# A second row buffer for the token scatter, 18 unread products, and a later copy of the experts' token numbers

## The chip, the cores and the metric

The kernel runs on one core of a Trainium2 chip. The metric is the device time of one execution in microseconds (us), the median of several runs. Profiles come from one execution that the hardware profiler recorded. Engines are named as in the profile: PE is TensorE's matrix products (PEld its weight loads), DVE is VectorE, ACT is ScalarE, POOL is GpSimd, SP is the engine whose queue issues most of the DMAs.

## What is computed

Three layers follow each other: attention that keeps the 32 largest scores of a row (2 batches, 8 heads, 576 positions, 64 per head), a dense layer with a cosine (1152 tokens, 512 to 2048 and back), and a mixture of 8 experts of which each token takes one.

```python
scores = scale * np.matmul(q, k.transpose(0, 1, 3, 2))
kth = np.partition(scores, -top_k, axis=-1)[..., -top_k:-top_k + 1]
scores = np.where(scores >= kth, scores, -1000000000.0)
attn = np.exp(scores - np.max(scores, axis=-1, keepdims=True))
attn = attn / (np.sum(attn, axis=-1, keepdims=True) + 1e-09)
x = np.matmul(attn, v)            # reordered to 1152 tokens x 512
h = x @ w_in
x = (h * np.cos(h)) @ w_out
...
expert_idx = np.argmax(x @ w_gate, axis=1)
# a token goes to row counts[e] of its expert's list, in order of token number
h = np.maximum(np.einsum('ecd,edf->ecf', disp, w1), 0.0)
y = np.einsum('ecf,efd->ecd', h, w2)
out[i] = gate_w[i] * y[expert_idx[i], pos[i]]
```

## The kernel before

**Stages.** Attention and the dense layer work on 9 tiles of 128 tokens, numbered 0 to 8 (tile 4 holds the ends of both batches). The dense layer takes the tiles in the groups [0], [1, 2], [3, 4], [5, 6] and [7, 8]. For a group, `layer_in` (L662) writes 512 columns of the hidden layer into `h`, ACT copies them to `hs` (L691), DVE and ACT form the cosine in `ur` (L695, L712), POOL multiplies (L720), and `layer_out` (L723) adds 16 products per tile into `x2` (L729).

**Routing.** `route` (L735) takes a finished tile of `x2`: ACT copies it into a row tile `xr` (L742), PE transposes it into `pt` (L660), ACT copies that to `gT` (L744), PE multiplies by the gate weights into `av` (L748), DVE picks the expert (L751 to L756), ACT takes the exponentials (L768), and DVE writes the gate weight beside the row (L760). `place` (L773) counts on PE how many earlier tokens chose each expert (L786), DVE makes row addresses `slot` from that (L789 to L792), and POOL scatters the 128 rows of `xr` to `xs` in DRAM by an indirect DMA (L795). Tile 4 has a row tile of its own, `xr4`, and is placed last, since it needs the counts of both batches. `largest` (L804) adds up all counts and lets DVE note whether a list is too long (L815 to L817, L831).

All tiles but 4 share the ring `xr`, and the ring `gT` and the PSUM ring `av` have one buffer each too.

**Experts.** `gather` (L949) loads an expert's rows from `xs` into `xg` by four DMAs, after all nine scatters. PE transposes them into `xp` (L964, L965), ACT and DVE split them into two parts `xgs` (L967, L968), and `expert_in` (L971) and `expert_out` (L997) run the two layers (products at L979, L981 and L1010). The result rows are scattered to the output (L1016) by token numbers, which DVE copies as integers from the gathered rows into `ti` (L959). Weights are loaded into `raw2` or `raw3` and split by ACT (L944) and DVE (L946).

**Order.** The class `Plan` records every operation with a cost, a rank and its dependencies; `emit` walks through time with these costs, picks for each engine the operation that can start first (the rank decides among those within 0.02 us), and writes out one fixed order per engine. Ring buffers are handed out there: an operation that needs a new buffer waits in the plan until one is free. On the chip every engine runs its queue strictly in this order and waits by semaphores. `forward` is written out twice: with `paired` true, which is what runs here, and as an exact version behind a test that isn't entered with these inputs.

The rings that the change touches, and the place of the token copy:

```python
    ring("xr", "mx", [128, RW], F32)
    ring("xr4", "mx", [128, RW], F32, tag="raw")
...
        P.dma(1.0, 1.6, ld, r=[("xs", t) for t in range(9)], w=[kx])
        P.op("dve", 0.1, lambda: DVE.tensor_copy(T["ti", e], T[kx][:, :, DM + 1]), r=[kx], w=[("ti", e)])
...
        R("rank", 90.0 + 10 * e - prm["ga"])
        gather(e)
```

Of the kernel before, what the change touches and what calls it, by code (L numbers as in the profile page):

```python
# [7 lines left out]
F32 = mybir.dt.float32  # L8
F32R = mybir.dt.float32r
BF = mybir.dt.bfloat16  # L10
# [9 lines left out]
T = B * S  # L20
DM = H * D
# [4 lines left out]
RW = 520  # L26
# [225 lines left out]
def forward(ctx, lasting, tc, kq, vn, vs_, w_in, w_out, w_gate, w1, w2, out, paired):  # L252
    nc = tc.nc
    PE, ACT, DVE, POOL, SP = nc.tensor, nc.scalar, nc.vector, nc.gpsimd, nc.sync
    prm = PRM if paired else FULL
    P = Plan(prm["tb"])
    T = P.T
# [13 lines left out]
    def ring(name, pool, shape, dtype, bufs=1, tag=None, gate=None):  # L271
        P.ring(name, lambda: pools[pool], shape, dtype, bufs, tag, gate)
# [5 lines left out]
    tri = lasting("tri", [128, 128], BF)  # L278
    ones = lasting("ones", [128, 128], BF)
    right = lasting("right", [128, 128], BF)  # L280
    iota8 = lasting("iota8", [128, 8], F32)
    tok = lasting("tok", [128, 9], F32)
    far = lasting("far", [128, 9], F32)
# [8 lines left out]
    counts = lasting("counts", [128, NE + 3], I32)  # L292
# [4 lines left out]
    CONST, MASKS = ("ident",), ("masks",)  # L297

    def iota(t, pattern, base, cm):
        POOL.iota(t, pattern=pattern, base=base, channel_multiplier=cm, allow_small_or_imprecise_dtypes=True)  # L300
# [14 lines left out]
    def masks():  # L315
        def go():
            iota(iota8, [[1, 8]], 0, 0)
            iota(tok[:, 0:4], [[128, 4]], 0, 1)
            iota(tok[:, 5:9], [[128, 4]], S, 1)
            iota(tok[0:64, 4:5], [[1, 1]], 512, 1)  # L320
            iota(tok[64:128, 4:5], [[1, 1]], S + 512, 1)
            iota(spare, [[1, 1]], int(OUT_OF_RANGE), 1)
            POOL.memset(ones, 1.0)
            POOL.tensor_scalar(far, tok, 1.0, OUT_OF_RANGE, op0=OP.add, op1=OP.mult)
            POOL.memset(right, 0.0)
            POOL.memset(right[:, 64:128], 1.0)
        P.op("pool", 1.2, go, w=[MASKS])
        P.dma(0.5, 0.3, lambda: SP.dma_start(wg, w_gate.rearrange("(c p) e -> p c e", p=128)), w=[("wg",)])
# [323 lines left out]
    ring("ur", "mx", [128, 2, 512], F32, 2, tag="ur")  # L652
    ring("nn", "mx", [128, 512], F32)
    ring("gT", "mx", [128, 512], F32)
    ring("xr", "mx", [128, RW], F32)
    ring("xr4", "mx", [128, RW], F32, tag="raw")

    def transposes(kp, src):
# [145 lines left out]
    def largest():  # L804
        kp = ("av", "total")

        def count():
            for t in range(9):
                PE.matmul(T[kp][:, 0:NE], ones, onehot[:, t], start=(t == 0), stop=(t == 8))
        P.op("pe", 0.1, count, r=[("pick", t) for t in range(9)] + [MASKS], w=[kp])  # L810

        m8, over, un = small[:, 8, 16:24], small[:, 8, 28:29], small[:, 8, 29:30]

        def tally():
            DVE.max(m8, T[kp][:, 0:NE])  # L815
            DVE.tensor_scalar(over, m8[:, 0:1], float(MAIN), None, op0=OP.is_gt)
            DVE.tensor_copy(counts[:, 0:NE], T[kp][:, 0:NE])  # L817
        P.op("dve", 0.3, tally, r=[kp, ("slot", 8)], w=[("counts", 0)])
        if not paired:
            P.op("dve", 0.1, lambda: DVE.tensor_copy(counts[:, NE:NE + 1], over), r=[("counts", 0)], w=[("counts", 1)])  # L820
            return
        kd = ("av", "doubts")
        P.op("dve", 0.4, lambda: (DVE.tensor_scalar(edge, edge, 0.0, 0.0, op0=OP.is_ge, op1=OP.add, accum_out=doubts[:, 0:1]),
                                  DVE.tensor_scalar(turns, turns, FEWER, 0.0, op0=OP.is_lt, op1=OP.add, accum_out=doubts[:, 1:2]),
                                  DVE.tensor_tensor(out=doubtb, in0=doubts[:, 0:1], in1=doubts[:, 1:2], op=OP.add)),
             r=[("edge", s) for s in range(NSTEPS)] + [("turns", t, g) for q in groups for t in q[:1] for g in range(2 * len(q))], w=[("doubts", 0)])
        P.op("pe", 0.1, lambda: PE.matmul(T[kd][:, 0:1], ones, doubtb, start=True, stop=True), r=[("doubts", 0), MASKS],
             w=[kd])
        P.op("dve", 0.2, lambda: (DVE.tensor_copy(counts[:, NE + 1:NE + 2], T[kd][:, 0:1]), DVE.tensor_copy(un, T[kd][:, 0:1])),
             r=[kd], w=[("counts", 2)])  # L830
        P.op("dve", 0.1, lambda: DVE.tensor_tensor(out=counts[:, NE:NE + 1], in0=un, in1=over, op=OP.add),  # L831
             r=[("counts", 0), ("counts", 2)], w=[("counts", 1)])


    R = P.__setattr__
    R("rank", -3.0)
# [30 lines left out]
    for q in groups:  # L867
        t, n = q[0], len(q)
# [24 lines left out]
                 table="exp")  # L893
    place(4)
    largest()
    all_first = range(len(P.ops))
    att = [i for i in all_first if any(k[0] in P.rings and P.rings[k[0]][0]() is pools["at"] for k in P.ops[i]["tiles"])]

# [29 lines left out]
    def wkey(q, e, i, a):  # L928
        return (q + "2" if e % 2 == 0 else q, (e, i, a))
# [19 lines left out]
    def gather(e):  # L949
        kx = ("xg", e)  # L950

        def ld():
            SP.dma_start(T[kx][:, 0, :], xs[e * CAP:e * CAP + 128, :])

            SP.dma_start(T[kx][:, 1, 0:DM], xs[e * CAP + 128:e * CAP + 256, 0:DM])
            for a in range(2):
                SP.dma_start(T[kx][64 * a:64 * a + 64, 1, DM:RW], xs[e * CAP + 128:e * CAP + MAIN, DM:RW])
        P.dma(1.0, 1.6, ld, r=[("xs", t) for t in range(9)], w=[kx])
        P.op("dve", 0.1, lambda: DVE.tensor_copy(T["ti", e], T[kx][:, :, DM + 1]), r=[kx], w=[("ti", e)])  # L959
        for c in range(4):  # L960
            kp, ks = ("xp", (e, c)), ("xgs", (e, c))

            def tr(c=c, kp=kp):
                PE.transpose(T[kp][:, 0:128], T[kx][:, 0, c * 128:(c + 1) * 128], ident)  # L964
                PE.transpose(T[kp][:, 128:256], T[kx][:, 1, c * 128:(c + 1) * 128], ident)  # L965
            P.op("pe", 0.25, tr, r=[kx], w=[kp], duty=0.5)
            P.op("act", 0.25, lambda kp=kp, ks=ks: ACT.activation(T[ks][:, 0], T[kp][:, 0:MAIN], AF.Copy), r=[kp], w=[ks])  # L967
            P.op("dve", 0.27, lambda kp=kp, ks=ks: DVE.tensor_tensor(  # L968
                out=T[ks][:, 1], in0=T[kp][:, 0:MAIN], in1=T[ks][:, 0], op=OP.subtract), r=[kp], w=[ks])
# [27 lines left out]
    def expert_out(e, a):  # L997


        kp, ko = ("yp", (e, a)), ("ot", (e, a))  # L1000
        for fc in range(8):
            ka, kb = wkey("wh", e, 4 + fc // 2, fc % 2), wkey("wl", e, 4 + fc // 2, fc % 2)

            def mm(fc=fc, ka=ka, kb=kb):
                h = T["hc", (e, fc)]
                hi, lo = h[:, 0:128], h[:, MAIN + 64:2 * MAIN]
                both = h[:, 128:256]
                uses = ((both, T[ka]), (both, T[kb])) if a else ((hi, T[ka]), (hi, T[kb]), (lo, T[ka]))
                for n, (x, w) in enumerate(uses):
                    PE.matmul(T[kp], x, w, start=(fc + n == 0), stop=(fc == 7 and n == len(uses) - 1))  # L1010
            P.op("pe", 0.463 if a else 0.695, mm, r=[ka, kb, ("hc", (e, fc))], w=[kp])

        rows = 64 if a else 128

        def scatter():
            st = POOL.indirect_dma_start(out=out, out_offset=bass.IndirectOffsetOnAxis(ap=T["ti", e][0:rows, a:a + 1], axis=0),  # L1016
                                         in_=T[ko][0:rows, :], in_offset=None, bounds_check=B * S - 1, oob_is_err=False)
            for x in outs:
                tc.declare_no_dep(st.ins, x.ins, reason="distinct tokens")
            outs.append(st)  # L1020

        def gates(r):
            return T["xg", e][r, a, DM:DM + 1]
        if a == 0:
            P.op("act", 0.55, lambda: ACT.activation(T[ko], T[kp], AF.Copy, scale=gates(slice(0, 128))),  # L1025
                 r=[kp, ("xg", e)], w=[ko])
        else:
            P.op("act", 0.55, lambda: ACT.activation(T[ko][0:64, :], T[kp][64:128, :], AF.Copy, scale=gates(slice(64, 128))),
                 r=[kp, ("xg", e)], w=[ko])
            P.op("dve", 0.6, lambda: DVE.scalar_tensor_tensor(  # L1030
                T[ko][0:64, :], T[kp][0:64, :], gates(slice(0, 64)), T[ko][0:64, :], op0=OP.mult, op1=OP.add),
                r=[kp, ("xg", e)], w=[ko])
        P.op("pool", 1.05, scatter, r=[ko, ("ti", e), ("filled",)], w=[("done", e, a)], lat=3.5)
# [103 lines left out]
```

## Time and profile before

| what | us |
|---|---|
| median of 3 runs | 698.27 (697.89 to 698.58) |
| the profiled execution | 697.17 |
| its span, first to last instruction | 695.4 |
| PE busy in it | 587.0 (84%) |
| DVE busy | 552.0 (79%) |
| ACT busy | 494.3 (71%) |
| POOL busy | 265.8 (38%) |

The profiled execution is 1.1 us below the median. Three stretches follow each other in it: up to about 410 us DVE and ACT are busy nearly all the time with attention; from there to 501 us PE is, with the last groups of the dense layer; from 530 us on PE is again, with the experts. Between 501 and 530 us no engine is busy for long: routing of the last tiles, their scatter, and the first gather lie there, one behind the other. Time in this stretch is read from the chain of waits and from the engines' own sequences, not from busy shares.

### The profile page before, as it was taken

What the parts mean: (1) busy time and instruction counts of PE and PEld (TensorE: products, weight loads), DVE (VectorE), ACT (ScalarE), POOL (GpSimd) and SP (SyncE); (2) the same over time, 40 slices, a digit from 0 to 9 for tenths busy, and PEclk for the clock granted to TensorE, in tenths of its full rate; (3) what the DMA queues carried; (4) which work ended last, traced back from release to release, by engine and by line L of the source; (5) the groups of instructions that cost most, each with busy time, mean ns of one, the idle gap of its engine ahead of it and who ended that gap; (6) DMA issues with size and microseconds to landing.
All of it is one profiled execution on the core that took longest, in us unless ns stands there. A gap on an engine that the chain in (4) does not pass through costs nothing.

```text
span 695.4 us, 11074 instructions
## 1 busy us (share of the span) xinstructions
PE 587.0 (84%) x3611; PEld 431.9 (62%) x3611; DVE 552.0 (79%) x1654; ACT 494.3 (71%) x1004; POOL 265.8 (38%) x316
## 2 busy tenths in 40 slices
PE   3333577799999999989999899999926999999994
PEld 1122355545776755866756567667425888999993
DVE  5999999999999999999999962555223888889630
ACT  4676998999799989787877764566313777778631
POOL 3466675677445545464544541322110101101111
PEclk9995658999899999999999999999956999999997
DMA  9543552064131201000000002353113677787300
GB/s 348 189 151 124 163 168 92 1 231 182 56 101 39 71 6 39 20 16 17 1 1 1 0 17 87 126 169 135 61 46 123 224 250 251 266 269 259 108 18 16
DMA packets 30786, 77.28 MB, mean 111 GB/s; under 512 B 4606, under 2 KB 4606, under 8 KB 30720
## 3 DMA queue, kind: packets, MB, share of 16 engines
q1 hardware_dynamic: 28976, 71.73, 30.7%
q0 software_dynamic: 1744, 4.76, 1.8%
q8 instruction: 30, 0.49, 0.3%
q14 instruction: 36, 0.29, 0.1%
HBM read 64.57 MB, written 12.69 MB: 111 GB/s over the span
## 4 chain that ended last, share of the span: by engine, by line
PE 40%; DVE 35%; ACT 15%; DMA 3%; issue 3%; POOL 1%; SPq 1%; POOLq 0%; DVEq 0%; ACTq 0%
PE yp L1010 11%; DVE W L513 9%; DVE C L517 8%; PE x L729 8%; PE hp L979 7%; DVE C L509 5%; PE hp L981 3%; ACT Sp L561 2%; DVE W L522 2%; ACT pen L556 2%; DVE wt L405 2%; ACT Sp L570 2%; ACT Sp L494 2%; PE h L684 2%; DVE Sp L574 2%
## 5 line engine op out<-in xcount | busy, mean ns | idle before, releaser
L729 PE MATMUL x<-wo,hs 128*128 128x512 f32 x288 | 138.2, 603 | 0.0
L559 POOL TENSOR_TENSOR Sp<-Sp,pen 128x576 f32<-128x576 f32 x72 | 98.9, 1373 | 63.9 <-ACT pen L556 63.3
L513 DVE MAX8 W<-C 128x8 f32<-128x288 f32 x288 | 118.2, 446 | 0.6
L946 DVE TENSOR_TENSOR wl<-raw,wh 128x512 fp32r<-128x512 f32 x128 | 89.9, 739 | 35.4 <-ACT wh L944 34.9
L517 DVE MATCH_REPLACE8 C<-W,C 128x288 f32<-128x288 f32 x216 | 93.8, 440 | 0.0
L589 PE MATMUL pt<-ident,Sp 128*128 128x128 f32 x324 | 56.4, 304 | 39.1 <-ACT Sp L570 32.5
L482 PE MATMUL S<-kq 64*128 64x288 f32 x256 | 57.8, 533 | 28.7 <-ACT Sp L494 19.8
L589 PEld LDWEIGHTS pt<-ident,Sp 128*128 128x128 f32 x324 | 40.0, 153 | 66.9 <-ACT Sp L570 42.1
L944 ACT ACTIVATE wh<-raw 128x512 fp32r<-128x512 f32 x128 | 74.0, 621 | 9.9 <-DMA raw<-in_w_dram 6.9
L684 PE MATMUL h<-xh,wh 128*128 128x256 f32 x256 | 78.1, 305 | 0.5 <-ACT hs L691 0.4
L979 PE MATMUL hp<-xgs,wh 128*128 128x384 f32 x256 | 76.3, 368 | 0.0
L729 PEld LDWEIGHTS x<-wo,hs 128*128 128x128 f32 x288 | 49.0, 190 | 43.5 <-issue 42.7
L1016 POOL DMA_INDIRECT out_dram<-ot,ti x16 | 16.6, 1035 | 152.8 <-ACT ot L1025 121.6
L685 PE MATMUL h<-xl,wh 128*128 128x256 f32 x256 | 71.9, 281 | 0.0
L686 PE MATMUL h<-xh,wl 128*128 128x256 f32 x256 | 71.8, 281 | 0.0
L1010 PE MATMUL yp<-wh,hc 128*128 128x512 f32 x192 | 68.4, 400 | 0.0
L509 DVE TENSOR_TENSOR C<-Sp 128x576 f32<-128x576 f32 x72 | 65.1, 904 | 3.0 <-ACT Sp L494 2.2
L720 POOL TENSOR_TENSOR hs<-hs,ur 128x512 f32<-128x512 f32 x36 | 48.4, 1356 | 46.4 <-ACT ur L712 45.0
L561 ACT ACTIVATE Sp<-Sp,tb 128x576 f32<-128x576 f32 x72 | 55.6, 773 | 14.2 <-POOL Sp L559 14.0
L981 PE MATMUL hp<-xgs,wl 128*128 128x192 f32 x256 | 65.3, 255 | 0.0
L556 ACT ACTIVATE pen<-Sp,tb 128x576 bf16<-128x576 f32 x72 | 55.2, 767 | 6.3 <-POOL tb L549 5.5
L591 ACT ACTIVATE PT<-pt 128x384 f32<-128x384 f32 x108 | 48.6, 483 | 12.2 <-PE pt L589 12.0
(138 smaller groups left out, 1365.8 us busy)
## 6 DMA issues: line engine op xcount, KB each, us to landing
raw<-in_w_dram SPq DMA_DIRECT2D x64, 512.0 KB, 3.8
wraw<-in_w_out_dram SPq DMA_DIRECT2D x16, 512.0 KB, 3.8
wraw<-in_w_in_dram SPq DMA_DIRECT2D x16, 512.0 KB, 4.0
xs<-z SPq DMA_DIRECT2D x1, 4680.0 KB
kq<-in_kq_dram SPq DMA_DIRECT2D x8, 576.0 KB, 5.7
v<-in_vn_dram SPq DMA_DIRECT2D x8, 320.0 KB, 6.2
v<-in_vs_dram SPq DMA_DIRECT2D x8, 320.0 KB, 3.3
out_dram<-z SPq DMA_DIRECT2D x1, 2304.0 KB
```

The lines of the kernel that those rows point to most:

```text
L509: DVE.tensor_tensor(out=T["C", s], in0=x[:, :, 0:HS], in1=x[:, :, HS:S], op=op)
L513: P.op("dve", 0.365, lambda r=r, i=i: DVE.max(T["W", s][:, i, LIST[r]:LIST[r] + 8], T["C", s][:, i, :]), r=[("C", s, i)], w=[("W", s, i)])
L517: P.op("dve", 0.42, lambda r=r, i=i: DVE.match_replace(T["C", s][:, i, :], T["W", s][:, i, LIST[r]:LIST[r] + 8], T["C", s][:, i, :], NEG), ...
L559: P.op("pool", 1.34, lambda i=i, kp=kp: POOL.tensor_tensor(out=T["Sp", s][:, i, :], in0=T["Sp", s][:, i, :], in1=T[kp], op=OP.subtract), r ...
L589: PE.transpose(T[kp][:, c * 128:(c + 1) * 128], P2[:, cc * 128:(cc + 1) * 128], ident)
L684: PE.matmul(o, hi, a, start=(kc == 0), stop=False, skip_group_check=True)
L729: P.op("pe", 0.86, lambda f=f, a=a: PE.matmul(T["x2", t], T[kh][:, a:a + 128], T["wo", 0][:, f, :], start=(f == 0), stop=(f == 15)), r=[kh ...
L944: P.op("act", 0.52, lambda a=a, hi=hi: ACT.activation(T[hi], T[kr][:, a * 512:(a + 1) * 512], AF.Copy), r=[kr], w=[hi])
L946: P.op("dve", 0.6, lambda a=a, hi=hi, lo=lo: DVE.tensor_tensor(out=T[lo], in0=T[kr][:, a * 512:(a + 1) * 512], in1=T[hi], op=OP.subtract), ...
L979: PE.matmul(T[kp][:, 0:2 * MAIN], T[ka][:, c:c + 128], x.rearrange("p a n -> p (a n)"), start=(kc == 0), stop=False, skip_group_check=True)
L981: PE.matmul(T[kp][:, 0:MAIN], T[kb][:, c:c + 128], x[:, 0], start=False, stop=(kc == 3), skip_group_check=True)
L1010: PE.matmul(T[kp], x, w, start=(fc + n == 0), stop=(fc == 7 and n == len(uses) - 1))
```

## The change

It has three parts.

- The ring `xr` gets two buffers.
- A new tile `awake` of 128 x 512 zeros in bfloat16 is set by POOL at the start, and a new function `stay_awake` puts 18 products of `ones` with it behind `largest`, in a tile of the ring `av`. Nothing reads the result. They depend on the first tally on DVE.
- The copy of the token numbers into `ti` is taken out of `gather` and recorded at the first half (`a == 0`) of `expert_out`, so that its rank is 96 + 10e instead of 90 + 10e - 4.016 in `paired`.

```diff
+    awake = lasting("awake", [128, 512], BF)
...
             POOL.memset(ones, 1.0)
+            POOL.memset(awake, 0.0)
...
-    ring("xr", "mx", [128, RW], F32)
+    ring("xr", "mx", [128, RW], F32, 2)
...
+    def stay_awake(n):
+
+        kp = ("av", "awake")
+
+        def mm():
+            for _ in range(n):
+                PE.matmul(T[kp], ones, awake, start=True, stop=True)
+        P.op("pe", 0.214 * n, mm, r=[MASKS, ("counts", 0)], w=[kp])
...
     place(4)
     largest()
+    if paired:
+        stay_awake(18)
...
         P.dma(1.0, 1.6, ld, r=[("xs", t) for t in range(9)], w=[kx])
-        P.op("dve", 0.1, lambda: DVE.tensor_copy(T["ti", e], T[kx][:, :, DM + 1]), r=[kx], w=[("ti", e)])
...
         kp, ko = ("yp", (e, a)), ("ot", (e, a))
+        if a == 0:
+            P.op("dve", 0.1, lambda: DVE.tensor_copy(T["ti", e], T["xg", e][:, :, DM + 1]), r=[("xg", e)], w=[("ti", e)])
```

The plan then writes other orders. ACT's queue at the end of routing; `xr_4963` and `xr_5005` are the row tiles of tiles 7 and 8. Before:

```order
L742 ACTIVATE xr_4963<-x2_4675 128x512
L744 ACTIVATE gT_4969<-pt_4968 128x512
L768 ACTIVATE small_87<-small_87 128x8
L742 ACTIVATE xr_5005<-x2_4754 128x512
L744 ACTIVATE gT_5010<-pt_5009 128x512
L768 ACTIVATE small_87<-small_87 128x8
L967 ACTIVATE xgs_5107<-xp_5101 128x192
```

Now (`xr_4965` is that of tile 7, `xr_4976` that of tile 8):

```order
L744 ACTIVATE xr_4965<-x2_4677 128x512
L744 ACTIVATE xr_4976<-x2_4762 128x512
L746 ACTIVATE gT_4971<-pt_4970 128x512
L746 ACTIVATE gT_4993<-pt_4992 128x512
L770 ACTIVATE small_88<-small_88 128x8 x2
L979 ACTIVATE xgs_5128<-xp_5122 128x192
```

The two tiles are now taken together, step by step, instead of one after the other.

PE's queue from the last product of the dense layer to the experts' first transposes (rows of the counts left out). Before:

```order
L729 MATMUL x2_4754<-wo_138,hs_4927 128x512 x2
L660 MATMUL pt_4968<-ident_75,xr_4963 128x128 x4
L748 MATMUL av_4975<-wg_86,gT_4969 128x8 x4
L786 MATMUL av_4987<-onehot_88,tri_76 128x8
...
L660 MATMUL pt_5009<-ident_75,xr_5005 128x128 x4
L748 MATMUL av_5016<-wg_86,gT_5010 128x8 x4
L786 MATMUL av_5028<-onehot_88,tri_76 128x8
...
L964 MATMUL xp_5101<-ident_75,xg_5085 128x128
```

Now:

```order
L731 MATMUL x2_4762<-wo_140,hs_4935 128x512 x2
L662 MATMUL pt_4970<-ident_75,xr_4965 128x128 x4
L750 MATMUL av_4981<-wg_87,gT_4971 128x8 x4
L662 MATMUL pt_4992<-ident_75,xr_4976 128x128 x4
L788 MATMUL av_4999<-onehot_89,tri_76 128x8
...
L750 MATMUL av_5018<-wg_87,gT_4993 128x8 x4
L788 MATMUL av_5030<-onehot_89,tri_76 128x8
...
L842 MATMUL av_5079<-awake_79,ones_77 128x512
...
L976 MATMUL xp_5122<-ident_75,xg_5106 128x128
```

Tile 8's transposes moved ahead of tile 7's count, and the 18 products stand between the counts and the first expert's transposes. Tile 6's transposes and gate products moved ahead as well, between products of the last group's `h`.

DVE's queue where the experts begin; `xg_5085` and `xg_5090` are the rows of experts 0 and 1. Before:

```order
L831 TENSOR_TENSOR counts_90<-small_87 128x1
L959 CAST ti_5099<-xg_5085 128x2
L968 TENSOR_TENSOR xgs_5107<-xp_5101,xgs_5107 128x192
L959 CAST ti_5112<-xg_5090 128x2
L968 TENSOR_TENSOR xgs_5110<-xp_5104,xgs_5110 128x192
L968 TENSOR_TENSOR xgs_5121<-xp_5114,xgs_5121 128x192
```

Now (experts 0 and 1 are `xg_5106` and `xg_5111`):

```order
L833 TENSOR_TENSOR counts_91<-small_88 128x1
L1014 CAST ti_5120<-xg_5106 128x2
L980 TENSOR_TENSOR xgs_5128<-xp_5122,xgs_5128 128x192
L1014 CAST ti_5133<-xg_5111 128x2
L980 TENSOR_TENSOR xgs_5131<-xp_5125,xgs_5131 128x192
L980 TENSOR_TENSOR xgs_5142<-xp_5135,xgs_5142 128x192
```

Both copies stand where they stood; those of the experts 2 to 6 moved back by four instructions, that of expert 7 stayed, and SP's queue is unchanged.

## Rows read from the trace of the kernel before

**Rows 1.** The chain of waits between 494 and 530 us: start, us, what.

```profile
494.19 6.97 PE x L729 x16
...
506.76 2.81 DMA xs<-xr,slot
509.67 0.61 ACT xr L742
...
517.41 4.03 DMA xs<-xr,slot x2
...
525.32 3.59 DMA xg<-xs
529.03 0.17 DVE ti L959
```

**Rows 2.** Busy time of PE, PEld, DVE, ACT, POOL by stretch, then PE's clock.

```profile
480.00:500.00 20.00, 20.00 (x73) 10.96 (x72) 8.03 (x15) 7.28 (x13) 5.45 (x6) 1.00 0.29 95
...
560.00:640.00 80.00, 80.00 (x467) 72.39 (x466) 68.40 (x196) 63.59 (x160) 8.35 (x8) 1.00 0.78 262
```

**Rows 3.** ACT in order of time: start, us, what, in brackets the idle time before.

```profile
499.62 0.60 ACT L742 ACTIVATE xr<-x 128x512 f32<-128x512 f32 x1 [8.19 <-PE x L729]
501.70 0.60 ACT L744 ACTIVATE gT<-pt 128x512 f32<-128x512 f32 x1 [1.48 <-PE pt L660]
...
509.67 0.60 ACT L742 ACTIVATE xr<-x 128x512 f32<-128x512 f32 x1 [4.78 <-DMA xs<-xr,slot]
```

**Rows 4.** PE in order of time, from the last routing to the first expert.

```profile
501.00 0.60 PE L660 MATMUL pt<-ident,xr 128*128 128x128 f32 x4
502.35 1.06 PE L748 MATMUL av<-wg,gT 128*128 128x8 f32 x8 [0.75 <-ACT gT L744]
...
512.18 1.88 PE L748 MATMUL av<-wg,gT 128*128 128x8 f32 x8 [0.75 <-ACT gT L744]
...
524.40 0.45 PE L964 MATMUL xp<-ident,xg 128*128 128x128 f32 x1 [7.21 <-DMA xg<-xs]
...
529.51 0.47 PE L964 MATMUL xp<-ident,xg 128*128 128x128 f32 x1 [2.28 <-DVE xgs L968]
...
533.68 0.57 PE L979 MATMUL hp<-xgs,wh 128*128 128x384 f32 x1
...
534.21 0.57 PE L979 MATMUL hp<-xgs,wh 128*128 128x384 f32 x1
```

**Rows 5.** DVE in order of time, in the same stretch.

```profile
505.30 0.15 DVE L789 SCALAR_TENSOR_TENSOR small<-av,onehot 128x8 f32<-128x8 f32 x1
...
517.51 0.16 DVE L817 CAST counts<-av 128x8 int32<-128x8 f32 x1
...
526.05 0.17 DVE L959 CAST ti<-xg 128x2 int32<-128x2 f32 x1 [8.27 <-DMA xg<-xs]
...
529.03 0.17 DVE L959 CAST ti<-xg 128x2 int32<-128x2 f32 x1 [2.55 <-DMA xg<-xs]
```

**Rows 6.** Stretches of half a microsecond around two changes of PE's clock.

```profile
504.00:504.50 0.50, 0.04 (x2) 0.04 (x2) 0.43 (x3) 0.01 (x1) 0.00 (x0) 0.58 0.00 0
...
534.50:535.00 0.50, 0.50 (x4) 0.50 (x4) 0.19 (x1) 0.28 (x1) 0.00 (x0) 0.70 0.00 0
```

**Rows 7.** Stretches of one microsecond around an earlier fall of the clock.

```profile
81.00:82.00 1.00, 0.34 (x4) 0.00 (x0) 1.00 (x4) 1.00 (x4) 0.19 (x1) 1.00 0.00 0
...
84.00:85.00 1.00, 0.00 (x0) 0.00 (x0) 1.00 (x7) 0.82 (x2) 1.00 (x2) 0.62 0.83 160
```

**Rows 8.** The chain of waits, 34 products of 512 columns.

```profile
543.97 7.91 PE yp L1010 x34
```

**Rows 9.** Tile 6's row copy on ACT.

```profile
466.84 0.60 ACT L742 ACTIVATE xr<-x 128x512 f32<-128x512 f32 x1 [1.42 <-DMA xs<-xr,slot]
```

**Rows 10.** Waits between 425 and 500 us: total, times, longest.

```profile
ACT wh L944 <- DMA raw<-in_w_dram: 6.9, 5, 2.7
```

**Rows 11.** The stretch after the masks, at the start of the program.

```profile
3.00:4.00 1.00, 0.00 (x0) 0.00 (x0) 0.00 (x0) 0.00 (x0) 0.00 (x0) 1.00 1.00 361
```

## The prediction

> **What bounds the kernel now.** I read the busy time by stretch first: PE has no idle moment from 480 to 500 us, nor in the 80 us from 560 to 640 [rows 2]. A microsecond saved on another engine there is worth nothing. Between these stretches the chain of waits [rows 1] shows one thing after another: the last product of `x2` ends at 494.19 + 6.97 = 501.16, tile 7 is routed and its scatter lands (506.76 + 2.81), only then ACT copies tile 8 at 509.67, tile 8 goes the same way, its scatter is issued at 517.41, the gathers follow, and the experts' products begin behind 529.5. Here a microsecond off the chain is a microsecond off the end, because what follows (gathers, weight loads behind them in SP's queue, experts) moves as one block.
>
> The sequence on ACT shows the one wait that a second row tile addresses: ACT stands for 4.78 us before tile 8's copy, until the scatter of the first row tile has landed [rows 3]. Tile 8's products had ended 8.5 us before (501.16 against 509.67).
>
> **The second row tile.** What it removes is not the 4.78 us alone, since tile 7's own routing also lay ahead of tile 8's. I follow the new order until tile 8's gate product, which started at 512.18 [rows 4].
> - Tile 7's copy stays at 499.62, tile 8's starts when PE has ended: 501.16 plus 0.17, the lag between the end of tile 7's last product (499.45, two products of tile 8 earlier, each two instructions of 6.97 / 16 = 0.43) and tile 7's copy. It ends at 501.93.
> - Tile 7's `gT` stood at 501.70 [rows 3] and now goes behind that copy: 0.2 us late. Its gate product moves from 502.35 to 502.55 and ends at 503.6.
> - Tile 8's transposes follow on PE, 0.60 us as tile 7's [rows 4]: 504.2. Its `gT` on ACT, 0.60 more with 0.1 of lag: 504.9.
> - `av` has one buffer. So tile 8's gate product also waits until DVE has read tile 7's count, at 505.30 + 0.15 before [rows 5]. With the 0.2 us it is 505.7, later than 504.9, and decides.
>
> Gain: 512.18 - 505.7 = **6.5 us**. From there to the gathers the steps and their order are those of before. Bounds: by 506 us PE ran at half clock before (below); if it still ran at the full level, the gate product would take 1.06 instead of 1.88 us [rows 4], which makes 7.3. If each of the four hand-overs lost another 0.25 us, it would be 5.5. POOL has no conflict: the scatters of 7 and 8 are then some 4 us apart, and one took 2.81 to land.
>
> The second buffer also lets tile 6 be routed earlier. Its copy waited for a scatter until 466.84 [rows 9]; now its transposes stand among PE's products from about 461 us. PE's work stays the same and fills its time, so this is worth 0, unless a product waits (last rival).
>
> The `awake` memset on POOL lies at the start, where no engine but the DMAs has work from 3 to 4 us [rows 11]. 0.
>
> **The 18 products.** No row shows a product of bfloat16 zeros. The nearest are products of 512 columns: 7.91 / 34 = 0.23 us each at the full level of the clock (2.4 GHz) [rows 8]. At the half level (1.2 GHz) the experts' first products come at 534.21 - 533.68 = 0.53 us for 384 + 192 columns [rows 4], thus 0.47 for 512. 18 of them take 4.2 or 8.5 us. They wait for DVE's cast of the counts, which ended at 517.67 [rows 5], and the first rows of an expert were there at 524.40 [rows 4]: a pause of 6.7 us, which moves along unchanged.
>
> Which level do they find? The clock fell at 504.08 (of the half microsecond from 504.0 a share of 0.16 was at the full level, mean 0.58) and rose at 534.80 [rows 6], 5.3 us after PE began to work steadily at 529.51. So the products start at half clock. If it rises 5.3 us after their start too, 5.3 / 0.47 = 11.3 are done by then, the other 6.7 take 1.5 us, and they end 6.8 us after their start, when the rows arrive. The transposes may lose some tenths, up to 8.5 - 6.7 = 1.8 us if the clock does not rise. Neither is on the path: DVE's copy of expert 1's token numbers waits until 529.03 [rows 5], the second split and the last transposes (529.51) stand behind it, and these transposes before had waited 2.28 us for DVE [rows 4].
>
> What they could give is the half clock at the experts' begin. From 529.51 to 534.80 PE ran at half level; at full level the same work takes half of 5.3, so **at most 2.6 us**. But it must hold from the end of the 18 products to 529.85 in old times, that is from 517.7 + 6.8 = 524.5 on, 5.3 us with only eight transposes in it. The rows say that it does not. After 501.16 four transposes and eight gate products ran, and the clock fell 2.9 us later [rows 6]; after 81.34 nothing ran, and it fell at 84.24, also 2.9 us later [rows 7]. I take **0**, and keep 2.6 for the range.
>
> One rule stands on the other side. The Trainium skill, page "TensorE: Matmul & The Clock Gate", section "Seeing it yourself", shows a run in which the clock fell 5.2 us after the last matmul. By that it would just about reach the experts' first product, and the sum would be 9.1 instead of 6.5 us. The rows of this case, 2.9 us twice, are the nearer evidence, but it gives the first rival more weight.
>
> **The copy of the token numbers.** One DVE instruction of 0.17 us per expert. The wait that matters is 2.55 us for expert 1's rows, in front of expert 0's second split [rows 5]. In the new queue that copy stands at the same place, behind expert 0's first split; the new rank changed nothing there, since the plan believed the rows to be there and DVE had nothing else to start. For the experts 2 to 6 the copy goes back by four instructions, in a stretch that PE fills [rows 2]. 0 in both.
>
> **Sum.** 6.5 + 0 + 0. Against the profiled execution: 697.17 - 6.5 = 690.7. That execution was 1.1 us faster than the median of its runs, and nothing in the chain above explains that, so I set the sum against the median: 698.27 - 6.5 = **691.8**. With the bounds of 5.5 and 7.3 it is 691.0 to 692.8.
>
> **Rivals.**
> 1. *The clock holds until the experts begin.* For it: the skill's 5.2 us, and the eight transposes in between, half a microsecond each at half level. Against it: the two falls after 2.9 us. 691.8 - 2.6 = 689.2. Chance 0.17.
> 2. *A wait takes the place of the one removed.* Tiles 7 and 8 meet in the single `av` and `gT`, and ACT's exponential of tile 7 stands behind tile 8's `gT`. If tile 8's gate product had to wait until tile 7's address is complete and the scatter is issued (506.76 [rows 1], 507 with the lag), the gain is 512.18 - 507 = 5.2, or 4 with a microsecond lost in the hand-overs: 693 to 694.3, 693.7 in the middle. Against it: the waits by data end at 505.7. Chance 0.07.
> 3. *Nothing gained.* Should the gathers hang on something else that ends at 521.7 as before, the time stays at 698.3. Against it: the chain names only the two scatters [rows 1]. Chance 0.02.
> 4. *Slower: PE's full stretch opens.* From 480 to 500 us PE was never idle [rows 2], so an idle microsecond there is added to the end. ACT's copies of tile 6 (row tile and `gT`, 1.2 us) now precede its copies of `h`, and `h` has one buffer. ACT also waits for weights, up to 2.7 us at a time [rows 10]. If that longest wait fell ahead of all four remaining copies of `h`, PE would lose 10.8 us: 698.27 - 6.5 + 10.8 = 702.6. It decides from 6.5 + 1.4 = 7.9 us on. Against it: three or more products of 0.87 us stand between the groups of `h` as cover. Chance 0.03.
>
> **How the numbers follow.** The forecast has the remaining 0.71. About 0.2% (1.4 us) is what a measurement of this kernel can tell from no change. Forecast and the first two rivals (0.95) lie beyond it on the fast side; I add a little to both others for what I overlooked. The range takes in the first rival with 0.4 us below it for the spread of the runs, and reaches to 693.4 above, past the forecast's own bound and half way into the second rival.
>
> **What would show it.** Right: in the new profile ACT's two row copies stand side by side near 500 and 501 us, without a wait for a scatter; the scatter of tile 8 is issued near 511 instead of 517.4; the 18 products run from about 511 to 518, the first half or more at half clock; PE's clock is at half again when the experts' products begin near 523, and rises about 5 us later; DVE still waits some 2.5 us for expert 1's copy. The clock step is wrong if those products come every 0.29 us from the first on. The first step is wrong if tile 8's gate product starts later than 506.5. The forecast as a whole would be wrong if `x2`'s last product ended later than 501.5 us.

## The result and the profile after

The changed kernel takes 691.59 us (median of 4 runs, 690.42 to 692.5), the kernel before beside it 698.14. The ratio is 0.9905, with a 95% interval of 0.9886 to 0.9923: 6.6 us or 0.95% faster, against a forecast of 691.8 in a range of 688.8 to 693.4. The profiled execution took 692.26, its span 690.5.

In that execution `x2` ended 1.8 us later than in the one shown of before (what goes with it, below). So places are compared by their distance from the end of `x2`'s last product, which was 501.16 and is 502.92. The chain of waits (start, duration, what; the answer to [rows 1]):

```profile
495.93 6.99 PE x L731 x16
502.94 0.60 ACT xr L744
...
505.72 0.60 ACT gT L746
...
507.29 1.86 PE av L750 x8
...
512.43 4.02 DMA xs<-xr,slot x2
516.70 0.33 SPq L966
...
520.33 3.61 DMA xg<-xs
524.06 0.17 DVE ti L1014
```

The scatter of tile 7, which stood in the chain of before ahead of tile 8's copy, is gone from it. From the end of `x2` to tile 8's gate product it is 4.37 us (before 11.02), to its scatter 9.51 (16.25). That takes 6.65 us off the gate product and 6.74 off the scatter. What follows kept its length: the gathers are issued 4.27 us behind the scatter (before 4.28). ACT in order of time (start, duration, line, what, in brackets the idle time before; [rows 3]):

```profile
501.22 0.60 ACT L744 ACTIVATE xr<-x 128x512 f32<-128x512 f32 x1 [8.21 <-PE x L731]
502.94 0.60 ACT L744 ACTIVATE xr<-x 128x512 f32<-128x512 f32 x1 [1.12 <-PE x L731]
503.43 0.59 ACT L746 ACTIVATE gT<-pt 128x512 f32<-128x512 f32 x1
505.72 0.60 ACT L746 ACTIVATE gT<-pt 128x512 f32<-128x512 f32 x1 [1.70 <-PE pt L662]
```

The second copy waits for PE alone. The 4.78 us for the scatter are not there. PE in the same stretch ([rows 4]):

```profile
504.08 1.06 PE L750 MATMUL av<-wg,gT 128*128 128x8 f32 x8 [0.74 <-ACT gT L746]
...
507.29 1.84 PE L750 MATMUL av<-wg,gT 128*128 128x8 f32 x8 [0.55 <-DVE small L791]
...
512.74 0.59 PE L842 MATMUL av<-awake,ones 128*128 128x512 bf16 x1 [0.53 <-DVE counts L819]
513.55 4.94 PE L842 MATMUL av<-awake,ones 128*128 128x512 bf16 x16 [0.22 <-issue]
519.51 0.30 PE L976 MATMUL xp<-ident,xg 128*128 128x128 f32 x1 [1.02 <-DMA xg<-xs]
...
524.54 0.48 PE L976 MATMUL xp<-ident,xg 128*128 128x128 f32 x1 [2.76 <-DVE xgs L980]
...
524.88 0.67 PE L991 MATMUL hp<-xgs,wh 128*128 128x384 f32 x1
525.35 0.36 PE L993 MATMUL hp<-xgs,wl 128*128 128x192 f32 x1
525.51 0.57 PE L991 MATMUL hp<-xgs,wh 128*128 128x384 f32 x1
...
526.04 0.57 PE L991 MATMUL hp<-xgs,wh 128*128 128x384 f32 x1
```

The 18 products (17 of them are in the records) end at 518.49, a microsecond before the rows they fill the time for. The products of the experts' first layer, `hp`, still come in pairs 0.63 and 0.53 us apart, the half level of the clock. DVE's copy of expert 1's token numbers waits as before ([rows 5]: 2.55 us):

```profile
506.97 0.16 DVE L791 SCALAR_TENSOR_TENSOR small<-av,onehot 128x8 f32<-128x8 f32 x1
...
524.06 0.17 DVE L1014 CAST ti<-xg 128x2 int32<-128x2 f32 x1 [2.78 <-DMA xg<-xs]
```

Half microseconds around the four changes of PE's clock, and PE in the stretch before (busy time of PE, PEld, DVE, ACT, POOL, then PE's clock; [rows 2, 6]):

```profile
480.00:500.00 20.00, 20.00 (x66) 10.27 (x65) 8.04 (x15) 7.84 (x14) 5.75 (x8) 1.00 0.32 105
...
505.50:506.00 0.50, 0.12 (x2) 0.00 (x0) 0.43 (x4) 0.28 (x1) 0.00 (x0) 0.98 0.00 0
...
516.00:516.50 0.50, 0.50 (x3) 0.25 (x2) 0.00 (x0) 0.00 (x0) 0.00 (x0) 0.78 0.01 0
...
523.00:523.50 0.50, 0.00 (x0) 0.00 (x0) 0.00 (x0) 0.00 (x0) 0.00 (x0) 0.54 0.97 352
529.50:530.00 0.50, 0.50 (x3) 0.50 (x3) 0.16 (x1) 0.31 (x1) 0.00 (x0) 0.63 0.00 0
```

A clock of 0.78 in a half microsecond means that a share of 0.56 of it was at the full level (0.56 x 1 + 0.44 x 0.5). So the clock fell at 505.98, 3.1 us after `x2`'s last product, rose at 516.22, fell again at 523.04, 4.55 us after the last of the 18 products, and rose at 529.87. The experts began 1.8 us after the second fall. PE has no idle moment from 480 to 500, as before.

### The profile page after: what moved, and what is told of

Read it like the earlier page. It is cut to its first block, busy times and chain, and to the rows that moved or that the text cites. A ratio compares the mean times of both kernels' runs of the same rounds, so it can differ in the third digit from the quotient of the medians.

```text
span 690.5 us, 11105 instructions
## 1 busy us (share of the span) xinstructions
PE 594.1 (86%) x3628; PEld 436.3 (63%) x3629; DVE 550.1 (80%) x1654; ACT 494.4 (72%) x1004; POOL 265.6 (38%) x317
## 4 chain that ended last, share of the span: by engine, by line
PE 43%; DVE 30%; ACT 19%; issue 2%; DMA 2%; POOL 1%; SPq 1%; POOLq 0%; DVEq 0%; ACTq 0%
PE yp L1024 11%; PE x L731 8%; DVE W L515 8%; PE hp L991 8%; DVE C L519 7%; DVE C L511 4%; PE hp L993 3%; ACT Sp L572 3%; ACT pen L558 3%; ACT Sp L563 3%; PE h L686 2%; ACT Sp L496 2%; DVE W L524 2%; PE h L687 2%; PE h L688 2%
## 5 line engine op out<-in xcount | busy, mean ns | idle before, releaser
L959 DVE TENSOR_TENSOR wl<-raw,wh 128x512 fp32r<-128x512 f32 x128 | 88.3, 727 | 33.5 <-ACT wh L957 32.5
```

What stands on the lines that cost most here:

```text
L959: P.op("dve", 0.6, lambda a=a, hi=hi, lo=lo: DVE.tensor_tensor(out=T[lo], in0=T[kr][:, a * 512:(a + 1) * 512], in1=T[hi], op=OP.subtract), ...
```

## The experiments

Theory: the second row tile is the whole gain, by the wait that left the chain; the 18 products and the token copy are worth nothing, each because one wait of DVE (2.78 us for expert 1's rows in this execution) stands in the same place. Rivals: the products carry part of it, or the copy does.

Ratios are to the kernel before, measured beside each run on the same chip; a ratio is not the quotient of the two medians named below, from which it differs by up to 0.2%. The runs of one kernel range over 0.7 to 5.8 us, so a difference of one microsecond is read from the traces. All times in the table are us from one trace each:

| kernel | ratio, 95% interval | `x2` end to gate product of tile 8 | `x2` end to first `hp` | first `hp` to PE's last product | clock at first `hp` |
|---|---|---|---|---|---|
| before | 1 | 11.02 | 28.69 | 156.50 | half, for 4.95 |
| copy_moved | 1.0001 (0.9983 to 1.0019) | 11.01 | 28.07 | 157.05 | half, for 6.0 |
| products | 1.0004 (0.9987 to 1.0020) | 11.02 | 27.83 | 155.57 | half, for 2.9 |
| after | 0.9905 (0.9886 to 0.9923) | 4.37 | 21.96 | 156.53 | half, for 5.0 |
| two_rows | 0.9911 (0.9890 to 0.9932) | 4.38 | 20.45 | 155.69 | half, for 2.9 |
| after_36 | 0.9859 (0.9837 to 0.9882) | 4.38 | 21.40 | 154.45 | full |
| late_copy | 0.9842 (0.9821 to 0.9864) | 4.38 | 18.20 | 154.66 | full |
| late_copy_none | 0.9858 (0.9833 to 0.9883) | 4.38 | 19.30 | 156.49 | half, for 4.4 |
| late_copy_23 | 0.9832 (0.9811 to 0.9853) | 4.39 | 18.93 | 154.99 | full |
| count_in_h | 0.9814 (0.9787 to 0.9840) | 3.72 | 18.29 | 154.67 | full |
| count_in_h_23 | 0.9826 (0.9797 to 0.9855) | 3.72 | 18.26 | 154.67 | full |
| count_in_h_none | 0.9865 (0.9838 to 0.9893) | 3.72 | 18.71 | 156.77 | half, for 5.0 |

### Each part alone

**two_rows** is the kernel before with one line changed:

```diff
-    ring("xr", "mx", [128, RW], F32)
+    ring("xr", "mx", [128, RW], F32, 2)
```

> The kernel before with the ring xr at two buffers and nothing else of the change. Theory: the second row tile is the whole gain; tile 8's gate product starts 4.4 us after x2's last product has ended (as in the changed kernel, 16.1 us less 11 in the kernel before), the gathers leave 6.7 us earlier, 691.6 us (0.991). Rival, the 18 products or the token copy carry a part of the gain: 693 us or more, with the gate product where the changed kernel has it but the experts later behind it.

Measured: 692.6 us (689.24 to 693.62), ratio 0.9911. The gate product stands where the changed kernel has it. PE in order of time:

```profile
502.42 1.06 PE L748 MATMUL av<-wg,gT 128*128 128x8 f32 x8 [0.74 <-ACT gT L744]
...
505.63 1.03 PE L748 MATMUL av<-wg,gT 128*128 128x8 f32 x8 [0.58 <-DVE small L789]
```

The whole gain is in this line, as far as intervals of 0.2% tell. In this execution the clock fell only at 507.50, so the gate product ran at the full level (1.03 instead of 1.84 us), and the scatter was issued 8.80 instead of 9.51 us after `x2`.

**products** is the changed kernel with one row tile and the copy back in `gather`:

```diff
-    ring("xr", "mx", [128, RW], F32, 2)
+    ring("xr", "mx", [128, RW], F32)
...
+        P.op("dve", 0.1, lambda: DVE.tensor_copy(T["ti", e], T[kx][:, :, DM + 1]), r=[kx], w=[("ti", e)])
...
-        if a == 0:
-            P.op("dve", 0.1, lambda: DVE.tensor_copy(T["ti", e], T["xg", e][:, :, DM + 1]), r=[("xg", e)], w=[("ti", e)])
```

> The changed kernel with one row tile again and the token copy back in gather, so that of the change only the 18 products and their memset are left. Theory: the products give nothing, since the clock is at half level again when the experts begin; tile 8's row copy waits 4 to 5 us for tile 7's scatter again; 698.1 us (1.000). Rival, the products keep the clock up into the experts' first products: up to 2.6 us less, 695.5 us, with the hp products 0.29 us apart from the first on.

Measured: 699.47 us beside 699.82, ratio 1.0004. ACT waits for the scatter again:

```profile
510.91 0.60 ACT L744 ACTIVATE xr<-x 128x512 f32<-128x512 f32 x1 [4.77 <-DMA xs<-xr,slot]
```

The last of its 18 products ended at 524.95, and the experts began at 530.24. PE, and the half microsecond just before the experts:

```profile
519.77 5.18 PE L842 MATMUL av<-awake,ones 128*128 128x512 bf16 x16 [0.22 <-issue]
...
530.24 0.67 PE L992 MATMUL hp<-xgs,wh 128*128 128x384 f32 x1
```

```profile
529.50:530.00 0.50, 0.10 (x1) 0.10 (x2) 0.50 (x3) 0.00 (x0) 0.00 (x0) 0.76 0.84 328
```

The clock fell at 529.76, half a microsecond before the products it should have served. So the products are worth nothing here by a narrow margin. That `hp` ran at the half level for 2.9 us instead of 4.95 is not shown to be their doing: in two_rows, without them, it is 2.9 too.

**copy_moved** has of the change only the token copy at its later place and the memset (one row tile, no products):

```diff
-    ring("xr", "mx", [128, RW], F32, 2)
+    ring("xr", "mx", [128, RW], F32)
...
-    if paired:
-        stay_awake(18)
```

> The changed kernel with one row tile and without the 18 products, so that of the change only the later place of the token copy is left (and the memset at the start). Theory: expert 1's copy stands where it stood in DVE's queue and waits 2.5 us for its rows; 698.1 us (1.000). Rival, the later copies of the experts 2 to 6 free DVE where PE waits for it: 0.3 us or more below.

Measured: 698.56 us beside 699.82, ratio 1.0001. DVE waits for expert 1's rows at the same place, here 1.54 us:

```profile
528.73 0.17 DVE L1012 CAST ti<-xg 128x2 int32<-128x2 f32 x1 [1.54 <-DMA xg<-xs]
```

Both rivals fall: alone, neither the products nor the copy move the time by more than their intervals of 0.2%. The wait itself differs from execution to execution: 2.55 us in the trace of before, 2.78 in after, 1.83 in products, 1.54 in copy_moved, 1.49 in two_rows. With it `hp` begins 11.6 to 12.5 us after tile 8's scatter is issued.

### The wait that was left, and what the products need

If DVE's wait for expert 1's rows is what makes the products worthless, taking it away should make them worth something. **late_copy** lets the token copy also wait for the first cut of `hc` of its own expert, so that it goes behind it in DVE's queue:

```diff
-            P.op("dve", 0.1, lambda: DVE.tensor_copy(T["ti", e], T["xg", e][:, :, DM + 1]), r=[("xg", e)], w=[("ti", e)])
+            P.op("dve", 0.1, lambda: DVE.tensor_copy(T["ti", e], T["xg", e][:, :, DM + 1]), r=[("xg", e), ("hc", (e, 0))], w=[("ti", e)])
```

> The changed kernel, with the token copy of each expert behind the first cut of hc of the same expert in DVE's queue, so that no copy stands between the two splits of expert 0. Theory: the wait of 2.8 us for expert 1's rows goes, the products hp begin 2.8 us earlier against x2's end (19.2 instead of 22.0 us), 688.8 us. If the clock, which fell 4.4 us after the 18 products, is then still up when hp begins, up to 2.4 us more: 686.4. Rival, hp then waits for the weights or for expert 0's second rows, and the wait only changes its name: 691.6 us.

Measured: 687.87 us beside 699.82, ratio 0.9842. On 698.1, the time of before that the expectation counts from, this is 687.1, between its two values. (Its 4.4 us for the fall behind the 18 products is 4.55 in the trace.) DVE in order of time:

```profile
521.45 0.62 DVE L980 TENSOR_TENSOR xgs<-xp,xgs 128x192 fp32r<-128x192 f32 x2 [0.63 <-ACT xgs L979]
...
524.22 0.16 DVE L1014 CAST ti<-xg 128x2 int32<-128x2 f32 x1
```

The copy no longer waits, and the splits follow each other. PE:

```profile
521.07 0.42 PE L991 MATMUL hp<-xgs,wh 128*128 128x384 f32 x1
521.33 0.25 PE L993 MATMUL hp<-xgs,wl 128*128 128x192 f32 x1
521.42 0.36 PE L991 MATMUL hp<-xgs,wh 128*128 128x384 f32 x1
```

`hp` begins 18.20 us after `x2` instead of 21.96, and its pairs come 0.35 us and then mostly 0.29 us apart: the full level from the first on. Of the 3.76 us, 2.78 are the wait and 0.8 tile 8's gate product, which happened to run at the full level here too. From tile 8's scatter to `hp` it is 9.40 us, 2.2 to 3.1 less than in the traces with the wait. The other 1.9 us come behind: from the first `hp` to PE's last product (below) it is 154.66 instead of 156.53. The five runs of late_copy (686.65 to 688.73) all lie below the six of two_rows on the same chip (689.24 to 693.62).

```profile
675.33 0.40 PE L1024 MATMUL yp<-wl,hc 128*128 128x512 f32 x1
```

**late_copy_none** is late_copy without the call of `stay_awake`:

```diff
-    if paired:
-        stay_awake(18)
```

> The late token copy of late_copy without the 18 products. In late_copy the clock had risen 3.8 us after the first of the 18 products, was still up when hp began 3.1 us after the last, and hp ran at the full level (0.29 us for a pair) from the first; its median was 3.7 us below that of the changed kernel in the earlier comparison, of which the wait removed is 2.8. Theory: without the products hp begins at half level for 3 to 6 us, which costs 1.6 to 3 us against late_copy: 0.988 of the kernel before. Rival, the products are worth nothing even here: 0.984, as late_copy.

Measured: 688.48 us beside 698.56, ratio 0.9858. PE:

```profile
521.77 0.67 PE L989 MATMUL hp<-xgs,wh 128*128 128x384 f32 x1
522.24 0.36 PE L991 MATMUL hp<-xgs,wl 128*128 128x192 f32 x1
522.40 0.57 PE L989 MATMUL hp<-xgs,wh 128*128 128x384 f32 x1
...
677.86 0.40 PE L1022 MATMUL yp<-wl,hc 128*128 128x512 f32 x1
```

The half level again, and 156.49 us to PE's last product. The expected 0.988 lies inside the interval, and so does late_copy's 0.984: these times alone do not tell the two apart, the traces do.

**late_copy_23** has 23 products instead of 18:

```diff
-        stay_awake(18)
+        stay_awake(23)
```

> late_copy with 23 products instead of 18. Theory: five more at the full level are 1.1 us, they end when expert 0's first rows land, and 18 already keep the clock up: 0.984, as late_copy, within 0.1%. Rival, the clock sometimes falls before hp in late_copy, and 23 close the gap: 0.982 and runs less spread. Other rival, the transposes come late behind the products: 0.985 or more, hp over 21.5 us after the rows' issue.

Measured: 686.49 us, ratio 0.9832. The products ended as the rows landed, and `hp` began 18.93 us after `x2`. That is 0.73 later than in late_copy because tile 8's gate product ran at the half level in this execution (1.85 us); from the scatter to `hp` it is 9.39 us, as there, so the five more products delay nothing. The distance to PE's last product is that of late_copy within 0.4 us, as the theory has it. The clock was already held by 18.

**after_36** leaves the wait and fills it: 36 products in the changed kernel.

```diff
-        stay_awake(18)
+        stay_awake(36)
```

> The changed kernel with 36 products instead of 18. Theory: at the full level they end about 3.9 us later than the 18, near 522.3 on the changed kernel's own times, ahead of the second split's end at 524.5, so they delay nothing, and the clock, which fell 4.4 us after the 18, is still up when hp begins: the half level at hp's begin goes, 2.4 us, 0.987. Rival, expert 0's first transposes stand behind them (519.5 before, now 522.3) and with them the first split, so that hp begins 1 us later and only 1.4 us are left: 0.989. Other rival, nothing changes: 0.9905.

Measured: 688.48 us beside 698.56, ratio 0.9859. PE:

```profile
511.14 9.58 PE L842 MATMUL av<-awake,ones 128*128 128x512 bf16 x36 [0.53 <-DVE counts L819]
520.82 0.30 PE L976 MATMUL xp<-ident,xg 128*128 128x128 f32 x1
...
522.70 0.42 PE L991 MATMUL hp<-xgs,wh 128*128 128x384 f32 x1
522.96 0.25 PE L993 MATMUL hp<-xgs,wl 128*128 128x192 f32 x1
523.05 0.36 PE L991 MATMUL hp<-xgs,wh 128*128 128x384 f32 x1
```

```profile
522.03 0.16 DVE L1014 CAST ti<-xg 128x2 int32<-128x2 f32 x1
```

The full level holds into the experts. The first transposes do stand behind the products, but `hp` begins 21.40 us after `x2`, no later than in the changed kernel: by then expert 1's rows have landed, so the copy on DVE does not wait. The rival that expected a microsecond's delay falls; from the scatter to `hp` it is 11.87 us, inside the 11.6 to 12.5 of the traces with the wait. This gives back what the 18 products missed: 154.45 us to PE's last product instead of 156.53. Since that is no longer than late_copy's 154.66, the still later token copies of the other experts, which late_copy has and after_36 has not, gave nothing that can be told.

### The single buffer of `av`, and the best of it together

**count_in_h** is late_copy with tile 7's count in another PSUM buffer that is free by then:

```diff
-        kp = ("av", ("p", t))
+        kp = ("h" if t == 7 else "av", ("p", t))
```

> late_copy with the count of tile 7 written into the buffer h, which is free by then, instead of av. Theory: tile 8's gate product does not wait for DVE's read of that count any more (0.58 us in late_copy) and begins right behind the count; everything behind it comes 0.5 to 0.6 us earlier, 0.983. Rival, DVE, which reads the count itself before it takes up tile 8's logits, is what tile 8 waits for next: no gain, 0.984.

Measured: 686.22 us beside 698.56, ratio 0.9814. PE:

```profile
504.94 1.06 PE L750 MATMUL av<-wg,gT 128*128 128x8 f32 x8 [0.74 <-ACT gT L746]
...
507.48 1.85 PE L750 MATMUL av<-wg,gT 128*128 128x8 f32 x8
```

Tile 8's scatter on POOL, here and in late_copy_none:

```profile
512.63 0.98 POOL L797 DMA_INDIRECT xs<-xr,slot  x1 [2.30 <-DVE small L817]
```

```profile
511.99 0.98 POOL L797 DMA_INDIRECT xs<-xr,slot  x1 [2.95 <-DVE small L817]
```

The gate product waits for nobody and starts 3.72 us after `x2` (503.76 here) instead of 4.38. At the same half level the scatter is issued 8.87 us after `x2`, in late_copy_none 9.52 (`x2` ends at 502.47 there). So the single buffer costs 0.65 us. In the median of five runs that is not resolved against late_copy.

**count_in_h_23** joins this with 23 products, **count_in_h_none** leaves the products out:

```diff
-        stay_awake(18)
+        stay_awake(23)
```

> Late token copy, tile 7's count in h, and 23 products: what helped in the other runs, together. Theory: gate product of tile 8 3.7 us after x2's end, no wait for expert 1's rows, hp at the full level from its first product, its begin to the end of the span 163.6 to 164.1 us as in the other kernels in which the clock was up there: 0.981. Rival, 23 products delay the first transposes and give back half a microsecond: 0.983.

> The same without the products. Theory: hp begins at half level, from its begin to the end of the span 165.5 to 167 us, 1.5 to 3 us longer than with the products: 0.984. Rival, what the products seemed to give was the spread of the runs: 0.981, as the kernel with them.

Measured: 686.63 us (0.9826) and 688.55 us (0.9865), both beside 698.02. From the first `hp` to PE's last product 154.67 and 156.77: the products are worth 2.1 us once the wait is gone. Here the times say so too: on the same chip all six runs with 23 products (683.04 to 687.62) lie below all five without (688.20 to 689.68), 1.9 us apart in the median. 23 instead of 18 are worth nothing that can be told, and they delay nothing (`hp` 18.26 and 18.29 us after `x2`), though the rival's 0.983 is as near to the ratio as the theory's 0.981. Theory and measurement differ by 0.2 to 0.3% in the two ratios, within their intervals. The lowest ratio is that of count_in_h, 1.9% below the kernel before and 0.9% below the changed one; late_copy, late_copy_23 and count_in_h_23 are not told apart from it.

## Why the prediction was right

**The second row tile: right, and nearly in size.** Forecast 6.5 us, with tile 8's gate product 4.54 us after `x2` (505.7 - 501.16). It stands at 4.37, the gain is 11.02 - 4.37 = 6.65, and the line alone gives the ratio of the whole change. The 0.2 us by which tile 7's `gT` was to come late are not there: tile 7's gate product starts 1.16 us after `x2`, before 1.19. The claim that DVE's read of tile 7's count decides, and not tile 8's `gT`, is in the rows (tile 8's `gT` ends at 506.32, the read at 507.13, the gate product starts at 507.29). count_in_h prices it at 0.66 us; the working had 505.7 - 504.9 = 0.8. The upper bound of 7.3, for a gate product at the full level, is what two_rows and late_copy show: the scatter 0.7 us earlier again.

**The 18 products: the result right, the two sizes behind it not.** The forecast was 0, since the clock would be at half again when the experts begin. So it was. But it rose 3.5 us after the products' start instead of 5.3, they ended after 5.75 us instead of 6.8, and it fell 4.55 us after their end instead of 2.9. The step that failed is the time of the fall: "2.9 us twice" was taken from falls behind other work, and behind these products it came 4.55 and 4.81 us later (after and products). Six transposes ran in between in both; whether they had a part in it no run separates. At the end of the program, where no product stands behind PE's last one, the clock fell 2.06 us after it in the traces of before and after and up to 5.24 us after it in count_in_h_none (683.82 against 678.58). So there is no fixed time, and the working took two falls out of a spread. With the gap as it was this changed nothing, but the margin was 1.8 us in the one and 0.5 us in the other, smaller than the 2.4 us of the working (529.85 - 524.5 - 2.9). That the forecast of 0 held is therefore in part luck: the gap was only a little longer than the clock held. The first rival was nearer than its reason against it said, and in late_copy, where the gap is 3.1 us, it is what happens. Its price was put at up to 2.6 us; measured it is 1.8 to 2.1 (156.49 to 154.66, 156.77 to 154.67).

The Trainium skill, page "TensorE: Matmul & The Clock Gate", section "Seeing it yourself", had 5.2 us after the last matmul. count_in_h_none agrees with it (5.24); in the other eleven traces the fall at the end of the program came sooner.

**The token copy: right.** copy_moved gives 1.0001, and the wait stayed. A gain of 0.3 us, as its rival has it, would be below what that interval tells. What the prediction did not ask is what that wait held up: with it gone, late_copy is 0.6% below the changed kernel, a part of which is the clock.

**The rivals.** A wait in place of the one removed would have put the gate product 5.8 us after `x2`; it is 4.37. PE's full stretch did not open (20.00 of 20 us). Nothing gained and slower are out by the interval.

**One sign was badly chosen.** The forecast was to be wrong if `x2` ended later than 501.5 us. It ended at 502.92, and the forecast held. The change is not the cause: products, with one row tile, ends `x2` at 502.41, and after_36, with two, at 501.30. What goes with it is PE's clock around 400 us. In the trace of after, of after_36, and of the kernel before:

```profile
400.00:404.00 4.00, 3.45 (x22) 3.45 (x22) 4.00 (x16) 2.67 (x6) 2.95 (x3) 0.57 0.02 6
```

```profile
400.00:404.00 4.00, 4.00 (x25) 2.82 (x25) 3.89 (x20) 3.97 (x9) 1.64 (x2) 1.00 0.04 8
```

```profile
400.00:404.00 4.00, 4.00 (x26) 2.81 (x24) 3.90 (x20) 3.97 (x9) 1.62 (x2) 1.00 0.04 8
```

Of twelve traces the four with a clock of 1.00 there and PE busy all the time end `x2` at 501.16 to 501.48. Those with 0.57 to 0.64 end it at 502.41 to 503.81. One with 0.76 ends it at 501.21, and late_copy, with 1.00 but PE idle for part of the stretch, at 502.87. In the seven traces in which the clock is at half level there, it fell between 398.49 and 401.10, and `x2` ends 102.4 to 102.7 us after that fall in all seven, the one with 0.76, which fell first, included. A place counted from the start of the program carries part of that. That the clock causes it was not tried. The prediction found no reason why the profiled execution of before lay 1.1 us below its median; that it is one of the four would fit, but the other runs have no trace.

## What to carry to other kernels

When a wait for a buffer leaves the critical chain, count from the last common event to the next resource that the two tiles share; here that was one PSUM buffer, and it set the gain to within 0.2 us. Work that keeps the clock up is worth something only if what follows begins soon enough behind it, so remove the wait between the two first, or fill it: with 18 products, one moved copy on DVE turned a gain of nothing into some 2 us, by the traces. Give signs of success as distances between events, not as times from the program's start.

## What the runs showed of the hardware

- Products of zeros in bfloat16 raised PE's clock: 3.4 to 4.2 us after the first of them in seven traces.
- After `x2`'s last product, with eight gate products and four transposes (one row tile) or eight (two) behind it, the clock fell 2.9 to 3.5 us later in ten traces and 6.2 us later in two (two_rows, late_copy). At the end of the program, with no product behind, it fell 2.1 to 5.2 us after PE's last one (twelve traces). One execution, or two, is a thin base for a time at which the clock falls.
- From the first `hp` to PE's last product the five traces at the full level take 154.45 to 154.99 us. 2.9 us at the half level at its begin cost 1.0 us (155.6 instead of 154.7), 4.4 to 6.0 us cost 1.8 to 2.4, which is less than half of the time at that level each time.
